# Lightning attention and an ELU mixture layer on one core: a third transpose buffer, a reordered block 11 and 12, a split last product, and output stores merged over two sequences

## The chip, the core and the metric

The kernel runs on one core of one Trainium2 chip. The metric is the device time of one execution in microseconds (us), lower is better. The kernel before takes 210.24 us, the median of three runs (209.36 to 210.96).

## What is computed

Attention with a decay per head, in blocks of 64 positions, and behind it a two-layer network with an ELU. The inputs are `q`, `k`, `v` of 4 sequences x 8 heads x 768 positions x 64, one decay `lam` per head, `w_in` of 512x2048 and `w_out` of 2048x512, all float32. Cut to what matters:

```
for b in range(nb):                       # nb = 12 blocks of 64 positions
    intra = (q_b @ k_b.T * Dmask) @ v_b   # Dmask: lam ** (i - j), lower half
    inter = (q_b * lam_pow) @ kv_state
    out_b = intra + inter
    kv_state = lam_block * kv_state + (k_b * rev_pow).T @ v_b
x = out.transpose(0, 2, 1, 3).reshape(4 * 768, 512)
h = x @ w_in
g = where(h > 0, h, exp(min(h, 0)) - 1)
return g @ w_out                          # 3072 x 512, float32
```

## The kernel before

**Blocks and groups.** The work is cut into 24 *blocks* `s` (0 to 23). Block `s` holds 64 positions of two neighbouring sequences, one on partitions 0 to 63, the other on 64 to 127: `where(s)` (L50) gives the first sequence, `2 * (s % 2)`, and the chunk of positions, `s // 2`. The state of block `s` is needed by block `s + 2`. Two blocks make one *group* of 256 rows; the two-layer network runs by groups.

**A block's attention.** `load` (L65) brings `k`, `q` and `v` from DRAM on POOL's queue, with a cast to fp16, in two DMAs each, one per sequence. Blocks 0 to 9 have `k` and `q` transposed on TensorE. From block 10 on `dma_T` (L234) does it with two DMA transposes on SP's queue, into a tile `TD` that has two buffers. `decay_q` (L205) scales the transposed `q` (tile `qs`), `decay_s` (L196) the state of the block two before (`sd`), `decay_v` (L187) the values (`vd`). `visit` (L278) issues the small matmuls of one block: state times `qs` (L304), scores of the *next* block from `TD` (L328), the state's update (L320), scores times values (L313). `att_P` (L214) masks the scores, `att_N` (L256) adds the update to `sd` and so makes the new state, `att_X` copies the block's output to `xt`, the input of the network.

**The network.** `mm1_h` (L377) computes one of eight units of a group's hidden layer: 8 matmuls of 128x256 into a PSUM bank `psH` (two buffers). `elu` (L420) makes `g` of it in one of two forms: for group 3 and units 0 to 4 of group 4, ACT reads the bank twice (L395, L397) and DVE combines two SBUF tiles (L402); for the rest ACT computes relu and exp (L429, L431) and DVE reads the bank itself (L432). Groups 0 to 2 have the second layer as plain products (`mm2`, L447), copied out by ACT in `mm2_o` (L457). Later groups use a form with seven half-size products (`part`, L516): each of 8 matmuls of 128x256 at L508, with sums of `g` (L490) and of the weights (L478) on DVE, and with `keep` (L535, ACT), `add` (L540, DVE) and `c2` (L544, DVE) to collect the output tile `o` (four buffers).

**Stores.** An output tile `o` of a block is 128 rows x 512 float32, 64 rows for each of two sequences, which lie 768 rows apart in DRAM. Each store is two DMAs of 64 rows (L461 in `mm2_o`, L527 in `store`), nearly all on SP's queue, in program order with the DMA transposes. Only at the end `c2` and the last `store` put one of their two halves on ACT's queue (L703, L706).

**What sets the order.** The order on each engine is written out by hand: a string of words for the first part (L565 to L579), and from L601 a loop over groups 3 to 11 and units `u` 0 to 7. A visit is made at `u` 1 and 5, so that group 4 has visits 10 and 11. Loads are issued at `u` 0 and 4, four blocks ahead. Block 11's decays are on DVE: `decay_s` at (4, 2), `decay_q` at (4, 3). From block 12 on both are on POOL, ahead of the visit before (L616, L617), behind all the loads that were issued until then. The last group's second layer stands by itself from L680 to L706.

Of the kernel before, what the change touches and what calls it, by code (L numbers as in the profile page):

```python
# [8 lines left out]
FP32 = mybir.dt.float32  # L9
# [7 lines left out]
def kernel(  # L17
# [35 lines left out]
    def half(x):  # L53
        return slice(64 * x, 64 * x + 64)
# [10 lines left out]
    def load(which, s):  # L65
        b, c = where(s)
        src, keep, tag = {"k": (k, kn, "kn"), "q": (q, qn, "qn"), "v": (v, vn, "vn")}[which]
        keep[s] = inp.tile([128, H, D], FP16, tag=tag, bufs=NB, name=f"{tag}{s}")
        for r in range(2):
            nc.gpsimd.dma_start(  # L70
                out=keep[s][half(r)],
                in_=src[b + r, :, c * L : (c + 1) * L, :].rearrange("h p d -> p h d"),
            )
# [122 lines left out]
    def decay_s(s, eng):  # L196
        if not NPR <= s < NS - NPR:
            return
        st[s]["sd"] = asb.tile([128, 2, NHP, D], FP32, tag="sd", bufs=3, name=f"sd{s}")
        eng.tensor_tensor(  # L200
            out=st[s]["sd"][:], in0=state[s - NPR][:],
            in1=lamL[:].unsqueeze(1).unsqueeze(3).broadcast_to([128, 2, NHP, D]), op=ALU.mult,
        )
# [18 lines left out]
    def att_C(s):  # L222
        if s >= NT:
            return
        T = asb.tile([128, 2, NHP, 2, L], FP16, tag="T", bufs=4, name=f"T{s}")
        to, psT = T[:].rearrange("p i j r t -> p r (i j) t"), st[s].pop("psT")
        if isinstance(psT, list):
            for r in range(2):
                nc.vector.tensor_copy(to[:, r], psT[r].rearrange("p (x t) -> p x t", t=L))
        else:  # L230
            nc.vector.tensor_copy(to, psT.rearrange("p r (x t) -> p r x t", t=L))
        st[s]["T"] = T

    def dma_T(s):  # L234
        if not NT <= s < NS:
            return
        T = asb.tile([128, 2, NHP, 2, L], FP16, tag="TD", bufs=2, name=f"TD{s}")
        for i, src in enumerate((kn, qn)):
            nc.sync.dma_start_transpose(
                out=T[:, i].rearrange("p j r t -> p j (r t)"),  # L240
                in_=src[s][:].rearrange("p h d -> p (h d)"),
            )
        st[s]["T"] = T
# [12 lines left out]
    def att_N(s):  # L256

        if s >= NS - NPR:
            return
        b, c = where(s)  # L260
        state[s] = asb.tile([128, 2, NHP, D], FP16, tag=f"st{b}", bufs=2, name=f"st{s}")
        to = state[s][:].rearrange("p y j d -> p y (j d)")
        if c:
            nc.vector.tensor_tensor(  # L264
                out=to, in0=psU, in1=st[s]["sd"][:].rearrange("p y j d -> p y (j d)"), op=ALU.add
            )
        else:
            nc.vector.tensor_copy(to, psU)
# [151 lines left out]
    def elu(grp, u):  # L420

        psH, nb, T, name = unit[grp, 0, 2, u]
        if grp == 3 or grp == 4 and u < 5:
            mm1_e(grp, 0, 2, u)
            mm1_g(grp, 0, 2, u, NF2)
            return

        r = msb.tile([128, nb, T], FP32, tag="r", bufs=4, name=f"r{name}")
        nc.scalar.activation(r[:], psH[:], AF.Relu, scale=-1.0)  # L429
        e = msb.tile([128, nb, T], FP32, tag="e", bufs=4, name=f"e{name}")  # L430
        nc.scalar.activation(e[:], r[:], AF.Exp, scale=-1.0)  # L431
        nc.vector.scalar_tensor_tensor(  # L432
            out=place(grp, 0, 2, u, 2, NF2), in0=e[:], scalar=-1.0, in1=psH[:],
            op0=ALU.add, op1=ALU.max,
        )
# [1 line left out]
    acc = {}  # L437
    nacc = [0]

    def rows(s, r):  # L440

        b, c = where(s)
        r0 = (b + r) * S + c * L
        return out[r0 : r0 + L, :]


    def mm2(s, n0):  # L447
        if n0 == 0:
# [8 lines left out]
    def mm2_o(s):  # L457
        o = msb.tile([128, DM], FP32, tag="o", bufs=4, name=f"o{s}")
        nc.scalar.copy(out=o[:], in_=acc.pop(s))
        for r in range(2):  # L460
            nc.sync.dma_start(out=rows(s, r), in_=o[half(r), :])  # L461

# [57 lines left out]
        }[i]  # L522
        product_of(grp, i, d[bank][:, cols], first, i in (4, 2, 3, 7))

    def store(s, o, cols, queues=(nc.sync, nc.sync)):
        for r in range(2):
            queues[r].dma_start(out=rows(s, r)[:, cols], in_=o[half(r), cols])  # L527

    def out_tile(grp, c):
        d = res[grp]  # L530
        if c not in d:
# [9 lines left out]
        o = out_tile(grp, c)[:, cols]  # L541
        nc.vector.tensor_tensor(out=o, in0=src, in1=res[grp][kept][:], op=ALU.add)

    def c2(grp, queues=(nc.sync, nc.sync)):  # L544
        d = res[grp]
        nc.vector.tensor_tensor(
            out=out_tile(grp, 1)[:].rearrange("p (i t) -> p i t", i=2),
            in0=d["A"][:, HD:].unsqueeze(1).broadcast_to([128, 2, HD]), in1=d["c45"][:].rearrange("p (i t) -> p i t", i=2), op=ALU.add,
        )
        store(2 * grp + 1, d[1], slice(0, DM), queues)  # L550

    def consts(i):
        if i == 0:
# [47 lines left out]
    for grp in range(3, NG):  # L601
        old, new = grp - 2, grp - 1
        for u in range(8):
            mm1_h(grp, 0, 2, u, NF2)
            s = 2 * grp + 2 + u // 4
            if s < NS and u % 4 == 0:

                if nload < NS:
                    load("k", nload)
                    load("q", nload)  # L610
                if nload <= NS:
                    load("v", nload - 1)
                    nload += 1
            if s < NS and u % 4 == 1:
                if s != 10:
                    decay_q(s + 1, nc.vector if s < 10 else nc.gpsimd)  # L616
                    decay_s(s + 1, nc.vector if s < 10 else nc.gpsimd)  # L617
                visit(
                    s, s if s < NS - NPR else None, s + 1 if s + 1 < NS else None,
                    s + 2 if s + 2 < NT else None,  # L620
                )
                dma_T(s + 3)

            if (grp, u) in five:
                mm2(5, 4 * five.index((grp, u)))
            end = grp == NG - 1
            if old >= 3 and u in (0, 2):
                part(old, {0: 3, 2: 7}[u])
            if new >= 3:
                at_u = {1: 2, 3: 4, 4: 1, 5: 5, 6: 6, 7: 3} if end else {3: 2, 4: 1, 5: 4, 6: 5, 7: 6}  # L630
                if u in at_u:
                    part(new, at_u[u])

            if old >= 3 and u == 1:
                add(old, 0, hi, res[old]["A"][:, hi], "p35")
                store(2 * old, res[old][0], slice(0, DM))
            if old >= 3 and u == 0:
                g_sum(old, 3)
            if new >= 3 and u in (4, 5, 6):
                g_sum(new, {4: 1, 5: 2, 6: 4}[u])  # L640
            if end and u == 3:
                g_sum(new, 3)
            if new >= 3 and u == 4:
                add(new, 0, lo, res[new]["A"][:, hi], "p2")
            if s + 1 < NS:
                if u % 4 == 1:
                    att_P(s + 1)
                if u % 4 == 2:
                    att_C(s + 2)
                    att_N(s)  # L650
                if u in (3, 7) and grp > 3:
                    decay_v(s + 1, nc.vector)
                if (grp, u) == (4, 2):
                    decay_s(s + 1, nc.vector)
                if (grp, u) == (4, 3):
                    decay_q(s + 1, nc.vector)
            if old >= 3 and u == 2:
                c2(old)
            if (grp, u) == (5, 0):
                w_sum(3, 1)  # L660
            elu(grp, u)
            if grp == 3 and u in (3, 6):
                decay_v(s + 1, nc.vector)
            if s < NS and u % 4 == 1:
                att_X(s, nc.scalar)
            if old >= 3 and u == 0:
                keep(old, "p35", res[old]["B"][:, hi])
            if new >= 3 and u == (1 if end else 3):
                keep(new, "p2", res[new]["B"][:, lo])
            if new >= 3 and u == (5 if end else 6):  # L670
                keep(new, "c45", res[new]["B"][:])
            if end and u == 6:
                keep(new, "u2", res[new]["A"][:, hi], 1)
            if end and u == 7:
                add(new, 0, hi, res[new]["B"][:, hi], "u2")
                store(2 * new, res[new][0], slice(0, DM))
            if (grp, u) == five[-1]:
                mm2_o(5)
# [20 lines left out]
    product_of(G, 2, M[1][:, lo], True, True)  # L699
    add(G, 0, lo, M[1][:, lo], "u1")  # L700
    store(2 * G, d[0], lo)
    part(G, 7)
    c2(G, (nc.sync, nc.scalar))  # L703
    part(G, 3)
    add(G, 0, hi, HB[:, hi], "u2")
    store(2 * G, d[0], hi, (nc.scalar, nc.sync))  # L706


# [28 lines left out]
```

## Time and profile before

| | |
|---|---|
| median of 3 runs | 210.24 us |
| the profiled execution's own time | 210.27 us |
| its span, from first to last instruction | 208.5 us |
| granted TensorE clock | 1.00 |
| TensorE (PE) busy | 91% of the span |
| VectorE (DVE) busy | 83% |
| ScalarE (ACT) busy | 68% |
| GpSimd (POOL) busy | 63% |
| last DVE instruction ends | 204.6 us into the span |

How to read the profile: times are us from the start of the span, those marked ns are nanoseconds. PE is the matmul array, PEld its weight load, SPq and ACTq are the instruction queues of SyncE and ScalarE where they issue DMAs. A group line names the line of the kernel, the engine, the operation, the tile written and the tiles read, the count behind an x, then busy time and mean ns of one, then the idle time in front and what ended it. A DMA's "us to landing" runs from its issue until its data is there. The share of a DMA queue is the time that its packets took, over the time of all 16 DMA engines; packets of one engine overlap, so that a share may be above 100%.

### The profile page before, as it was taken

The page shows a single profiled execution, that of the slowest core. Times are in us where ns is not written, and L with a number is a line of the kernel's source. Part 1 is how long each engine was busy: PE and PEld are TensorE (multiplying, and loading weights), DVE is VectorE, ACT ScalarE, POOL GpSimd, SP SyncE. Part 2 cuts the span into 40 slices and gives each one's busy share as a digit, 9 for nine tenths or more (in the row PEclk, how much of TensorE's full clock was granted, in tenths as well). Part 3 has the DMA queues.
Part 4 walks back from the last instruction along what each step waited for, and adds up shares of the span by engine and source line. Part 5 has one row for each costly group of instructions (what it writes and reads, how often), then busy time and mean ns, then how long its engine had stood idle before and what let it go on. Part 6 is the DMA issues. An engine that isn't in the chain of part 4 may idle for free.

```text
span 208.5 us, 7848 instructions
## 1 busy us (share of the span) xinstructions
PE 190.2 (91%) x3352; PEld 158.1 (76%) x3352; DVE 172.1 (83%) x281; ACT 140.7 (68%) x265; POOL 132.0 (63%) x180
## 2 busy tenths in 40 slices
PE   0448989999999999989999999999999999999991
PEld 0347977846776777868888888888888888888880
DVE  3677596798989898999989999999979956758672
ACT  5314686741784878767878778778788688877820
POOL 8978933899899879964999999999412200000000
PEclk9999999999999999999999999999999999999999
DMA  6999999999999999999999999999924404004043
GB/s 103 145 152 134 169 200 196 179 118 170 109 148 153 168 115 162 114 74 108 126 170 90 151 163 72 190 116 91 189 29 57 101 0 105 5 6 94 3 101 101
DMA packets 99731, 24.38 MB, mean 117 GB/s; under 512 B 92400, under 2 KB 96752, under 8 KB 99696
## 3 DMA queue, kind: packets, MB, share of 16 engines
q0 software_dynamic: 78208, 13.38, 96.0%
q1 hardware_dynamic: 20128, 10.03, 25.5%
q10 hardware_dynamic: 1360, 0.46, 1.2%
q8 instruction: 26, 0.43, 0.8%
q14 instruction: 9, 0.07, 0.1%
HBM read 27.27 MB, written 6.29 MB: 161 GB/s over the span
## 4 chain that ended last, share of the span: by engine, by line
PE 83%; DVE 6%; POOL 3%; DMA 3%; issue 2%; ACT 1%; DVEq 0%; POOLq 0%
PE psH L385 40%; PE psM L508 22%; PE psM L452 10%; DMA wi<-in_moe_w_in_dram 3%; PE psO_None L304 2%; PE psZ L328 2%; POOL vn L70 1%; DVE g L432 1%; PE psO_None L313 1%; PE psHA L508 1%; PE psHB L508 1%; PE psZ L320 1%; DVE s L490 1%; DVE vd L191 1%; DVE P L217 1%
## 5 line engine op out<-in xcount | busy, mean ns | idle before, releaser
L385 PE MATMUL psH<-xt,wi 128*128 128x256 f16 (+1 forms) x960 | 101.8, 257 | 2.6 <-DMA wi<-in_moe_w_in_dram 1.7
L385 PEld LDWEIGHTS <-wi 128*128 128x128 f16 x960 | 80.7, 101 | 13.7 <-issue 2.7
L432 DVE SCALAR_TENSOR_TENSOR g<-e,psH 128x512 f16<-128x512 f32 x59 | 40.2, 682 | 12.5 <-ACT e L431 12.1
L429 ACT ACTIVATE r<-psH 128x512 f32<-128x512 f32 x59 | 35.2, 597 | 21.5 <-PE psH L385 21.4
L431 ACT ACTIVATE e<-r 128x512 f32<-128x512 f32 x59 | 37.2, 630 | 1.9
L70 POOL DMA_DIRECT2D qn<-in_q_dram x46 | 32.4, 727 | 5.3 <-issue 2.7
L70 POOL DMA_DIRECT2D vn<-in_v_dram x48 | 34.0, 734 | 2.6 <-DMA qn<-in_q_dram 1.0
L395 ACT ACTIVATE e<-psH 128x512 f32<-128x512 f32 x37 | 22.2, 599 | 19.1 <-PE psH L385 18.8
L70 POOL DMA_DIRECT2D kn<-in_k_dram x46 | 32.5, 725 | 2.3 <-DMA wo<-in_moe_w_out_dram 2.3
L508 PEld LDWEIGHTS <-s 128*128 128x128 f16 x288 | 28.1, 98 | 3.4
L402 DVE SCALAR_TENSOR_TENSOR g<-e,r 128x512 f16<-128x512 f32 x37 | 26.1, 713 | 5.2 <-ACT r L397 5.2
L209 POOL TENSOR_TENSOR qs<-TD,powi 128x512 f16<-128x512 f16 x12 | 15.8, 1316 | 17.3 <-PE psO_None L304 12.4
L508 PE MATMUL psM<-wt,s 128*128 128x256 f16 x192 | 24.9, 273 | 0.0
L452 PE MATMUL psM<-wo,g 128*128 128x512 f16 x96 | 23.9, 380 | 0.0
L508 PEld LDWEIGHTS <-g 128*128 128x128 f16 x216 | 20.5, 98 | 2.6
L397 ACT ACTIVATE r<-psH 128x512 f16<-128x512 f32 x37 | 22.1, 598 | 0.0
L191 DVE TENSOR_TENSOR vd<-vn,rev 128x512 f16<-128x512 f16 x22 | 19.6, 891 | 0.0
L217 DVE TENSOR_TENSOR P<-psZ,mask 128x512 f16<-128x512 f32 x24 | 16.4, 684 | 2.6 <-PE psZ L328 2.0
L508 PE MATMUL psM<-wo,g 128*128 128x256 f16 x136 | 17.6, 273 | 0.0
L252 ACT CAST xt<-psO_None 128x512 f16<-128x512 f32 x20 | 11.5, 577 | 6.2 <-PE psO_None L313 6.2
L264 DVE TENSOR_TENSOR st<-psZ,sd 128x512 f16<-128x512 f32 x20 | 13.7, 683 | 0.9 <-PE psZ L320 0.9
L200 POOL TENSOR_TENSOR sd<-st,lamL 128x512 f32<-128x512 f16 x10 | 13.4, 1345 | 1.4 <-DVE st L264 1.4
(77 smaller groups left out, 207.0 us busy)
## 6 DMA issues: line engine op xcount, KB each, us to landing
out_dram<-o SPq DMA_DIRECT2D x45, 128.0 KB, 3.4
vn<-in_v_dram POOLq DMA_DIRECT2D x48, 64.0 KB, 4.6
kn<-in_k_dram POOLq DMA_DIRECT2D x46, 64.0 KB, 4.5
qn<-in_q_dram POOLq DMA_DIRECT2D x46, 64.0 KB, 4.9
wi<-in_moe_w_in_dram POOLq DMA_DIRECT2D x8, 256.0 KB, 5.8
wo<-in_moe_w_out_dram POOLq DMA_DIRECT2D x4, 512.0 KB, 7.7
kraw<-in_k_dram SPq DMA_DIRECT2D x2, 128.0 KB, 4.1
qraw<-in_q_dram ACTq DMA_DIRECT2D x2, 128.0 KB, 4.5
```

The costliest lines, as they stand in the source:

```text
L70: nc.gpsimd.dma_start(out=keep[s][half(r)], in_=src[b + r, :, c * L : (c + 1) * L, :].rearrange("h p d -> p h d"),)
L191: eng.tensor_tensor(out=st[s]["vd"][:], in0=vn[s][:], in1=rev[:].unsqueeze(2).broadcast_to([128, H, D]), op=ALU.mult,)
L217: nc.vector.tensor_tensor(out=d["P"][:].rearrange("p y j t -> p y (j t)"), in0=psS, in1=mask[:].rearrange("p y j t -> p y (j t)"), op=ALU. ...
L385: nc.tensor.matmul(psH[:, i, :], lhsT=wi[n // 4][:, kk, (n % 4) * 128 : (n % 4 + 1) * 128], rhs=xt[grp][:, kk, c0 * 128 : c0 * 128 + T], s ...
L395: nc.scalar.activation(e[:], psH[:], AF.Exp)
L397: nc.scalar.activation(r[:], psH[:], AF.Relu)
L402: nc.vector.scalar_tensor_tensor(out=place(grp, c0, nc_, n0, nb, step), in0=e[:], scalar=-1.0, in1=r[:], op0=ALU.add, op1=ALU.min,)
L429: nc.scalar.activation(r[:], psH[:], AF.Relu, scale=-1.0)
L431: nc.scalar.activation(e[:], r[:], AF.Exp, scale=-1.0)
L432: nc.vector.scalar_tensor_tensor(out=place(grp, 0, 2, u, 2, NF2), in0=e[:], scalar=-1.0, in1=psH[:], op0=ALU.add, op1=ALU.max,)
L452: nc.tensor.matmul(acc[s], lhsT=g_of(s, n), rhs=wo[n // 4][:, n % 4, :], start=(n == 0), stop=(n == NFT - 1),)
L508: nc.tensor.matmul(to, lhsT=lhsT, rhs=rhs, start=start and n == 0, stop=stop and n == NF2 - 1, skip_group_check=True,)
```

## The change

- `TD` gets three buffers.
- In group 4, `att_N(10)` stands at unit 1 in place of 2, and `decay_s(11)` behind `decay_q(11)` at unit 3 in place of 2. Unit 4 of group 4 takes the second form of the ELU.
- At (4, 4) POOL issues: load k of block 15, `decay_q(12)`, loads q 15, v 14 and k 16, `decay_s(12)`. Before it was k 15, q 15, v 14, `decay_q(12)`, `decay_s(12)`, and k 16 at (5, 0).
- Every store is one DMA: its source is 128 rows of a tile, its destination in DRAM 2 x 64 rows.
- The last product (part 3 of group 11) is made in two halves of 128 columns, the first into `HB`, the second into `M[1]` with a precomputed addend `w`; each has its own add. The last stores are one on ACT's queue (`c2`) and one on SP's.

```diff
-        T = asb.tile([128, 2, NHP, 2, L], FP16, tag="TD", bufs=2, name=f"TD{s}")
+        T = asb.tile([128, 2, NHP, 2, L], FP16, tag="TD", bufs=3, name=f"TD{s}")
...
-        if grp == 3 or grp == 4 and u < 5:
+        if grp == 3 or grp == 4 and u < 4:
...
-    def rows(s, r):
+    def store(s, o, cols, queue=nc.sync):
         b, c = where(s)
-        r0 = (b + r) * S + c * L
-        return out[r0 : r0 + L, :]
+        queue.dma_start(
+            out=out.rearrange("(b t) d -> b t d", b=B)[b : b + 2, c * L : (c + 1) * L, cols],
+            in_=o[:, cols],
+        )
...
-        for r in range(2):
-            nc.sync.dma_start(out=rows(s, r), in_=o[half(r), :])
+        store(s, o, slice(0, DM))
...
-    def store(s, o, cols, queues=(nc.sync, nc.sync)):
-        for r in range(2):
-            queues[r].dma_start(out=rows(s, r)[:, cols], in_=o[half(r), cols])
...
-                if nload < NS:
+                if (grp, u) == (4, 4):
                     load("k", nload)
+                    decay_q(s + 1, nc.gpsimd)
+                    load("q", nload)
+                    load("v", nload - 1)
+                    load("k", nload + 1)
+                    decay_s(s + 1, nc.gpsimd)
+                elif nload < NS:
+                    if grp != 5 or u:
+                        load("k", nload)
                     load("q", nload)
                 if nload <= NS:
-                    load("v", nload - 1)
+                    if (grp, u) != (4, 4):
+                        load("v", nload - 1)
                     nload += 1
             if s < NS and u % 4 == 1:
-                if s != 10:
+                if s not in (10, 11):
                     decay_q(s + 1, nc.vector if s < 10 else nc.gpsimd)
                     decay_s(s + 1, nc.vector if s < 10 else nc.gpsimd)
...
                 if u % 4 == 2:
                     att_C(s + 2)
+                if (grp, u) == (4, 1) or u % 4 == 2 and s != 10:
                     att_N(s)
...
-                if (grp, u) == (4, 2):
-                    decay_s(s + 1, nc.vector)
                 if (grp, u) == (4, 3):
                     decay_q(s + 1, nc.vector)
+                    decay_s(s + 1, nc.vector)
...
     store(2 * G, d[0], lo)
+    w = msb.tile([128, HD // 2], FP32, name="w")
+    nc.vector.tensor_tensor(
+        out=w[:], in0=d["u2"][:, HD // 2 :], in1=d["c45"][:, HD + HD // 2 :], op=ALU.add
+    )
     part(G, 7)
-    c2(G, (nc.sync, nc.scalar))
-    part(G, 3)
-    add(G, 0, hi, HB[:, hi], "u2")
-    store(2 * G, d[0], hi, (nc.scalar, nc.sync))
+    c2(G, nc.scalar)
+    for i, (bank, more) in enumerate(((HB, d["u2"][:, 0 : HD // 2]), (M[1], w[:]))):
+        c = slice(HD + i * HD // 2, HD + (i + 1) * HD // 2)
+        for n in range(NF2):
+            nc.tensor.matmul(
+                bank[:, c], lhsT=gs[G, 4][:, n, :], rhs=wo[2 + n // 4][:, n % 4, c],
+                start=i == 1 and n == 0, stop=n == NF2 - 1, skip_group_check=True,
+            )
+        nc.vector.tensor_tensor(out=out_tile(G, 0)[:, c], in0=bank[:, c], in1=more, op=ALU.add)
+    store(2 * G, d[0], hi)
```

More of the change, by code (lines that the diff above doesn't have):

```diff
@@ L542, in add, with c2 @@
         nc.vector.tensor_tensor(out=o, in0=src, in1=res[grp][kept][:], op=ALU.add)
-    def c2(grp, queues=(nc.sync, nc.sync)):
+    def c2(grp, queue=nc.sync):
         d = res[grp]
@@ L549, in c2 @@
         )
-        store(2 * grp + 1, d[1], slice(0, DM), queues)
+        store(2 * grp + 1, d[1], slice(0, DM), queue)
     def consts(i):
```

## The prediction

> **What bounds the kernel now.** I read the chain of waits first, then the waits around blocks 10 to 12, which the change reorders, then the DMA view by stretches, because every store changes its form, and last the chain at the end. The page and its chain:
>
> ```profile
> span 208.5 us, 7848 instructions
> ...
> PE 190.2 (91%) x3352; PEld 158.1 (76%) x3352; DVE 172.1 (83%) x281; ACT 140.7 (68%) x265; POOL 132.0 (63%) x180
> ...
> PE 83%; DVE 6%; POOL 3%; DMA 3%; issue 2%; ACT 1%; DVEq 0%; POOLq 0%
> ```
>
> TensorE bounds it: 83% of the chain, and the steady groups repeat every 14.7 us without a gap. The chain of the stretch 80 to 96 us leaves PE for DVE once, at visit 11 (PE would go on at 88.4) and the unit after it:
>
> ```profile
> 87.60 0.85 DVE vd L191
> 88.45 0.60 DVE qs L209
> ...
> 92.32 0.68 DVE g L432
> 93.00 0.05 issue
> 93.05 1.05 PE psH L385 x8
> ```
>
> The waits from 74 to 95 us say what PE loses there:
>
> ```profile
> PE psO_None L304 <- DVE qs L209: 0.7, 1, 0.7
> ...
> PE psH L385 <- DVE g L432: 0.5, 1, 0.5
> ```
>
> So the middle holds 1.2 us to be won. Now the DMA view. From 41 to 47 us only POOL's loads run:
>
> ```profile
> q0 software_dynamic: 5686, 0.71, 187.5%
> ```
>
> 5,686 packets in 6.0 us on 16 engines are 16.9 ns each; the share of 187.5% shows that packets overlap two deep, so shares are not occupancy. Then 45 to 85 us, and 85 to 152 us, where the loads end:
>
> ```profile
> q0 software_dynamic: 27814, 3.46, 159.4%
> q1 hardware_dynamic: 4144, 2.23, 29.9%
> ...
> out_dram<-o SPq DMA_DIRECT2D x12, 128.0 KB, 4.4
> ```
> ```profile
> q0 software_dynamic: 27939, 3.47, 109.2%
> q1 hardware_dynamic: 11679, 4.72, 39.2%
> ...
> out_dram<-o SPq DMA_DIRECT2D x16, 128.0 KB, 3.7
> ```
>
> Loads alone are 27,814 / 16 x 16.9 ns = 29.4 us of each engine in the first 40 us, and 29.5 us in the next 67. From 160 us on there are almost only stores:
>
> ```profile
> q1 hardware_dynamic: 2144, 2.56, 23.6%
> ...
> out_dram<-o SPq DMA_DIRECT2D x17, 128.0 KB, 2.4
> ```
>
> The chain's last pieces; the last add ends at 204.6, and 3.9 us of stores follow:
>
> ```profile
> 202.34 0.87 PE psHA L508 x8
> 203.21 0.89 PE psHB L508 x8
> ...
> 204.19 0.42 DVE o L542
> ```
>
> **The change, part by part.** The sum is made against the profiled execution's 210.27 us (208.5 of span, 1.8 around it), 0.03 above the median of 210.24.
>
> *Third buffer.* SP's queue waits 8.9 us for two `qs` reads on DVE: 3.5 before the transposes of block 12 (from 73.9 to 77.5) and 5.4 before block 13's (83.7 to 89.1). Both go. `TD` 12 can land near 81, 13 near 91 in place of 96.6. POOL's idle 4.7 us at 92 to 96.7 goes, but nothing on the chain waits for POOL there (that `qs` ends at 98.3, its visit is at 104.5): worth nothing by itself.
>
> *Block 11 on DVE.* Before `qs` 11 stood: masked scores, g, state, sd, g, vd. Now: masked scores, state, g, g, vd. One `sd` (0.60 apart in the timeline) goes behind it, so visit 11 starts up to 0.60 earlier; `sd` 11 is needed only at 93.5. The state 10 comes one g earlier, that g 0.6 later; it ends before 85, and g is read two groups of products later, so this costs nothing. Unit 4 in the other ELU form has DVE instead of ACT free the bank: 0 to 0.5 (the row above for unit 5); I take 0, DVE being ahead by the 0.6.
>
> *Block 12 on POOL.* `qs` 12 moves ahead of loads q 15, v 14 (2.7 us of issue) and of k 16 (1.4, from behind `sd` 12). At 82.0 it would wait if `TD` 12 is late; with the third buffer it lands at about 81, so nothing; without cover it costs what holds four to six loads, up to the 2.9 us by which it lands later today (84.9), hidden by the loads' lead below. `sd` 12 (1.5) comes after k 16, near 88, still 9 us before its update. DVE instructions beside today's 84.9 to 87.9 pair of POOL took 1.65 and 1.52 in place of 0.68; such lengthening moves, it doesn't go. I take the two waits, 0.6 + 0.5 = 1.1, as gained; bounds 0 and 1.8.
>
> *Last product.* 16 matmuls of 128 columns for 8 of 256: the 128-column row runs 16 in 0.89 us, beside 0.87, so 0. The first add runs beside the second half; the last add is 128 columns, about 0.3 for 0.42; `w` (0.3) lies under the product before. One issue of 0.55 goes from each queue. Together 0.3 gained; bounds 0 and 0.9.
>
> *Merged stores.* 24 tiles, 128 rows per DMA instead of 64. No row shows this form: every transfer of the trace has an outermost count of 64 or 128 on both sides, and each 64-row store leaves 64 packets of 2,048 bytes and 16 closing ones of 4 bytes in the trace's DMA records. The new destination's outermost loop counts 2, with a jump of 768 rows. Lower bound: spread over 16 engines as now, one issue of about 0.59 us less per tile on SP, which is idle: 0. Upper bound: one engine per sequence, two in all. Then a tile is 64 rows on each. In the trace's DMA records such rows follow 80 ns apart on an engine with nothing else to do: 5.1 us. The last stretch's share gives the other end: 23.6% of 16 x 48.5 us for 2.56 MB is 18.7 us of engine time per 0.262 MB, 9.4 on each of two, but with overlap counted twice. I take two engines and 5.1. The reason is a judgement on form: to stay on 16, the transfer would have to be cut inside a loop whose outer step jumps, and a cut along the outermost loop accounts for all that the rows show.
>
> On two engines this has two prices. *Loads:* both engines must carry 29.4 + 6 tiles x 5.1 + 6 transposes x 0.5 (32 packets of some 16 ns) = 63 us in the first 40, and 29.5 + 8 x 5.1 + 22 x 0.5 = 81 in the next 67: 37 too much. Loads have a lead of 8 us (block 12: issued at 67.2, its scores at 89.1, less 1.4 + 4.7 + 2.5 + 4.9 for issue and landing of load and transpose) to 13 (block 14, likewise); I take 11. Transposes stand behind the stores on SP's queue, so the rest shows as `visit` waiting for `TD`: +27. *The end:* from 200.6 (the store issued at 198.6, 2 us to its data) come three full tiles and two half-row ones: 3 x 5.1 + 2 x 64 x 46 ns = 21.3 us, ending at 222.6 with its completion: +14.
>
> The sum: 210.3 + 27 + 14 - 1.1 - 0.3 = 249.9, so 250 us. With 9.4 per tile the same steps give 327, too far up for rows that overlap; with 6.7 (105 ns, the spacing beside other traffic) 279.
>
> The Trainium skill, "DMA: Bandwidth & Descriptors", section "Why a DMA increments its semaphore by 16 and not by 1", says that a transfer uses the largest number of engines up to 16 that divides both sides' outermost counts, which here is 2. By it the sum stays 250; by the row of 64-row stores alone it would be 209. The same page's "Rules for kernel authors" advises one 128-partition transfer instead of two on disjoint halves, which by itself speaks for the merge; no run shown here tells the two apart.
>
> **Rivals.**
>
> *Only the end is hurt* (25%). Two engines, but loads keep going ahead of stores and transposes ahead of need. For it: output tiles have four buffers, so stores may lag two groups; a steady group has 14.7 us for 10.2 of stores. Against: the first stretch is over by 23 us, and transposes queue behind stores. 210.3 + 14 - 1.4 = 223.
>
> *Sixteen engines, the other side* (25%). The store is spread as now; then only the waits and the last product count: 210.3 - 1.4 = 208.9, not slower. It decides from eight engines on: 16 rows each, 1.3 us a tile, 14 x 0.6 more on each engine, which both stretches can hold (29 of 40 us used). For it: nothing in the trace runs on fewer engines. Against: nothing in it has an outermost count of 2.
>
> *POOL is held up* (within the last): `TD` 12 is late, POOL stands at `qs` 12 with q 15, v 14 and k 16 behind it, whose transposes wait. Up to 2.9, less the 8 of lead: 0, and visible only as POOL idle. No chance of its own.
>
> **How the numbers follow.** The forecast (two engines, loads delayed) has 50%, its own range 237 to 279 (from a lead of 13 with two stores in arrears, 37 - 13 - 10 = 14 in place of 27, to rows 105 ns apart). About 1%, 2.1 us, is what a measurement of this kernel can tell from no change. Sixteen engines: 208.9 is 0.7% below, so of its 25% I give 15 to within 1%, 9 to faster (a gain of over 2.1 needs the upper bounds 1.8 and 0.9), 1 to slower. Slower: 50 + 25 + 1 = 76%. The range must reach to sixteen engines to leave no more than 2 in 10 out: 208 to 270 holds some 42 + 25 + 20.
>
> **What would show it.** Right: the stores' time to landing 8 us or more where it is 3.4 now, loads and transposes above 6; PE waiting for `TD` from visit 9 on; the last add near 236 and 15 to 18 us from it to the end. The middle: PE's waits for `qs` 11 and g gone, SP's wait for `qs` gone. Wrong: stores landing in 3 us. If they land late but TensorE's steady group stays 14.7, it is 223.

## The result

The changed kernel takes 272.98 us, the median of 4 runs, beside 210.03 for the kernel before. The ratio is 1.281, with a 95% interval of 1.268 to 1.295: 59 us slower. Single executions of a kernel can come out a few per cent longer than the others: ratios leave those out, while medians, spreads and some traces include them (the trace below is one of 278.31 us, where the ratio rests on 267.88 and 270.50). So prices are taken from ratios, and the trace is read for places and shares.

### The profile page after: what moved, and what is told of

It reads as the page before. It is cut to its first block, busy times and chain, and to the rows that moved or that the text cites. A ratio compares the mean times of both kernels' runs of the same rounds, so it can differ in the third digit from the quotient of the medians.

```text
span 276.5 us, 7824 instructions
## 1 busy us (share of the span) xinstructions
PE 205.2 (74%) x3360; PEld 166.0 (60%) x3360; DVE 172.9 (63%) x283; ACT 141.9 (51%) x265; POOL 131.3 (47%) x180
## 4 chain that ended last, share of the span: by engine, by line
PE 43%; DMA 26%; POOL 10%; issue 9%; DVE 3%; ACT 1%; SPq 0%; POOLq 0%
PE psH L385 20%; PE psM L508 18%; DMA wo<-in_moe_w_out_dram 7%; DMA vn<-in_v_dram 7%; DMA TD<-qn 4%; DMA kn<-in_k_dram 3%; POOL qn L70 3%; POOL kn L70 3%; POOL vn L70 3%; DMA wi<-in_moe_w_in_dram 2%; DMA qn<-in_q_dram 2%; DVE s L490 1%; POOL wi L88 1%; PE psO_None L304 1%; PE psHA L508 1%
## 5 line engine op out<-in xcount | busy, mean ns | idle before, releaser
L385 PE MATMUL psH<-xt,wi 128*128 128x256 f16 (+1 forms) x960 | 109.0, 268 | 4.1 <-DMA wi<-in_moe_w_in_dram 2.2
L385 PEld LDWEIGHTS <-wi 128*128 128x128 f16 x960 | 84.6, 105 | 18.9 <-issue 5.4
L432 DVE SCALAR_TENSOR_TENSOR g<-e,psH 128x512 f16<-128x512 f32 x60 | 40.9, 682 | 17.0 <-ACT e L431 16.4
L70 POOL DMA_DIRECT2D qn<-in_q_dram x46 | 32.0, 711 | 24.5 <-DMA kn<-in_k_dram 20.3
L508 PEld LDWEIGHTS <-s 128*128 128x128 f16 x280 | 28.9, 104 | 4.8
L402 DVE SCALAR_TENSOR_TENSOR g<-e,r 128x512 f16<-128x512 f32 x36 | 24.4, 686 | 8.9 <-ACT r L397 8.9
L508 PE MATMUL psM<-wt,s 128*128 128x256 f16 x192 | 27.8, 293 | 0.0
L191 DVE TENSOR_TENSOR vd<-vn,rev 128x512 f16<-128x512 f16 x22 | 16.9, 770 | 13.9 <-DMA vn<-in_v_dram 13.9
L453 PE MATMUL psM<-wo,g 128*128 128x512 f16 x96 | 25.6, 400 | 0.0
L335 PEld LDWEIGHTS <-qn 64*64 64x64 f16 x160 | 3.2, 125 | 24.0 <-DMA qn<-in_q_dram 11.0
L320 PE MATMUL psZ<-vd,kn 64*64 64x64 f16 x352 | 7.6, 201 | 11.1 <-issue 10.9
```

The lines of the kernel that those rows point to most:

```text
L70: nc.gpsimd.dma_start(out=keep[s][half(r)], in_=src[b + r, :, c * L : (c + 1) * L, :].rearrange("h p d -> p h d"),)
L191: eng.tensor_tensor(out=st[s]["vd"][:], in0=vn[s][:], in1=rev[:].unsqueeze(2).broadcast_to([128, H, D]), op=ALU.mult,)
L385: nc.tensor.matmul(psH[:, i, :], lhsT=wi[n // 4][:, kk, (n % 4) * 128 : (n % 4 + 1) * 128], rhs=xt[grp][:, kk, c0 * 128 : c0 * 128 + T], s ...
L402: nc.vector.scalar_tensor_tensor(out=place(grp, c0, nc_, n0, nb, step), in0=e[:], scalar=-1.0, in1=r[:], op0=ALU.add, op1=ALU.min,)
L432: nc.vector.scalar_tensor_tensor(out=place(grp, 0, 2, u, 2, NF2), in0=e[:], scalar=-1.0, in1=psH[:], op0=ALU.add, op1=ALU.max,)
L453: nc.tensor.matmul(acc[s], lhsT=g_of(s, n), rhs=wo[n // 4][:, n % 4, :], start=(n == 0), stop=(n == NFT - 1),)
```

## The profile after

The page: TensorE's share of the span falls from 91% to 74%, and of the chain from 83% to 43%. In its place stand DMA, POOL and "issue", which is time in front of an instruction for which the profile shows no releaser.

```profile
span 276.5 us, 7824 instructions
...
PE 205.2 (74%) x3360; PEld 166.0 (60%) x3360; DVE 172.9 (63%) x283; ACT 141.9 (51%) x265; POOL 131.3 (47%) x180
...
PE 43%; DMA 26%; POOL 10%; issue 9%; DVE 3%; ACT 1%; SPq 0%; POOLq 0%
```

The chain from 20 to 104 us says which transfers are late. A load of `v` takes 19.4 us where the median was 4.6, and the second transpose of block 11 (`TD<-qn`) 12.1:

```profile
49.15 19.43 DMA vn<-in_v_dram
...
75.57 9.23 DMA kn<-in_k_dram
84.81 0.03 issue
84.83 0.02 POOLq L70
84.85 0.49 issue
85.34 5.07 DMA qn<-in_q_dram
90.41 0.35 SPq L239
90.76 0.04 issue
90.80 0.03 SPq L239
90.83 0.03 issue
90.86 12.09 DMA TD<-qn
```

TensorE's first new wait is for `q` of block 7, which it transposes at L335 and whose loads were issued at 47.8 and 48.5 us. Later in the trace it stands in the middle of visits for something that the profile doesn't name (from the waits of the whole run; L320 is the state's update):

```profile
PE psO L335 <- DMA qn<-in_q_dram: 10.8, 2, 7.6
...
PE psZ L320 <- issue: 10.9, 2, 5.5
```

The DMA view of 45 to 85 us: 15,067 packets of loads in place of 27,814 in the same 40 us, and loads that need twice their time. The merged stores have no time to landing in this view, so they are followed by their packets below.

```profile
q0 software_dynamic: 15067, 1.87, 121.0%
q1 hardware_dynamic: 1034, 1.17, 14.3%
...
kn<-in_k_dram POOLq DMA_DIRECT2D x12, 64.0 KB, 10.3
qn<-in_q_dram POOLq DMA_DIRECT2D x11, 64.0 KB, 10.2
```

The end: the last add stops at 257.5, and 19.0 us of stores follow in place of 3.9. From 258 us on, the DMA view has a flat rate of about 50 GB/s, which is what two engines give with a row of 2,048 bytes each 80 ns (51 GB/s); the fullest slices of the kernel before, with the same tiles, have some 200 GB/s.

```profile
257.18 0.29 DVE o L723
```
```profile
GB/s 53 53 53 44 53 53 53 44 53 53 53 53 44 53 53 53 49 49 53 53 53 47 53 49 46 51 47 49 49 49 49 49 49 49 46 49 20 0 0 0
```

Visits by the start of their last matmuls (L313), us, from the traces; the last five rows belong to the experiments below:

| kernel | visit 5 | 6 | 9 | 11 | 12 | 22 | 23 | last add ends | span |
|---|---|---|---|---|---|---|---|---|---|
| before | 55.7 | 62.1 | 76.7 | 89.5 | 98.0 | 171.8 | 178.3 | 204.6 | 208.5 |
| changed | 55.7 | 76.0 | 96.9 | 113.9 | 123.3 | 224.8 | 231.4 | 257.5 | 276.5 |
| e3, merged at the end only | 55.5 | 61.9 | 76.4 | 88.5 | 98.6 | 172.1 | 178.6 | 204.8 | 223.6 |
| e7, all stores on ACT's queue | 55.9 | 85.4 | 105.8 | 118.1 | 128.4 | 218.3 | 227.2 | 255.8 | 274.6 |
| e9, merged for blocks 0 to 5 | 55.9 | 74.4 | 93.9 | 107.4 | 119.9 | 195.0 | 201.6 | 227.7 | 231.7 |
| e10, merged for blocks 6 to 19 | 55.0 | 61.3 | 76.2 | 88.2 | 99.5 | 201.4 | 207.9 | 234.0 | 238.0 |
| e11, split and first ELU form | 57.4 | 63.8 | 78.6 | 90.7 | 102.7 | 176.2 | 182.7 | 208.8 | 212.9 |

Three places: 14 us at once between visits 5 and 6 and 11 more up to visit 12, then groups of 20.3 us on average ((224.8 - 123.3) / 5) where they were 14.8, and the end.

## The experiments

Theory: a merged store runs on two DMA engines, which delays loads and transposes in the middle and the closing stores at the end. Rivals: the reordering of blocks 11 and 12 is to blame; only the end is hurt; it is not the count but the jump in the destination, or the number of DMAs, that makes stores slow.

**Which part of the change it is: e1 and e2.** e1 is the changed kernel with each store as two DMAs again:

```diff
-        queue.dma_start(
-            out=out.rearrange("(b t) d -> b t d", b=B)[b : b + 2, c * L : (c + 1) * L, cols],
-            in_=o[:, cols],
-        )
+        for r in range(2):
+            r0 = (b + r) * S + c * L
+            queue.dma_start(out=out[r0 : r0 + L, cols], in_=o[half(r), cols])
```

> The changed kernel with one thing undone: each store is again two DMAs of 64 rows. Theory (a merged store runs on two DMA engines): all of the loss goes, 208 to 210 us, stores land in about 3 us and leave 16 closing packets each. Rival (the reordering of blocks 11 and 12 or the third buffer makes POOL and the loads late): it stays above 250 us.

Measured: 211.05, ratio 0.998 (0.993 to 1.002), so all of the loss goes; it is a little above the 208 to 210 expected, because the small gains of the change aren't there either. e2 is the kernel before with the opposite edit, the merged store and nothing else but the queues of the last two stores.

> The kernel before with the merged store alone; c2's last store on ACT's queue, the last one on SP's. Theory: about the changed kernel's time, 262 to 278 us, TensorE waiting for k, q and TD from about 50 us on. Rival (the reordering): 209 to 212 us.

Measured: 273.58, ratio 1.278 (1.265 to 1.291). The merged store is the whole loss, within the intervals, and the rest of the change is worth nothing that can be measured.

**Middle and end: e3 and e4.** Both are the changed kernel; `store` merges only under a condition, and else issues the two DMAs of e1:

```diff
+        if s >= 20:        # e3; e4: s < 20
             queue.dma_start(
                 out=out.rearrange("(b t) d -> b t d", b=B)[b : b + 2, c * L : (c + 1) * L, cols],
                 in_=o[:, cols],
             )
+            return
```

> The changed kernel, stores merged for blocks 20 to 23 alone. Theory: the loads' price goes and the end's stays, the last add at 203 to 205 us and 15 to 19 us behind it, 221 to 226 us in all. Rival (the end is hidden, all the loss is in the middle): 208 to 211 us.

Measured: 225.40, ratio 1.067 (1.060 to 1.074), so 14.2 us (12.6 to 15.7) for the end. The chain stops as early as in the kernel before, and two engines work on alone: in the DMA view from 205 us on the rate is again flat.

```profile
204.46 0.29 DVE o L728
```
```profile
GB/s 53 48 48 53 53 53 44 53 53 53 53 53 44 53 53 53 53 44 53 53 53 53 44 51 53 48 48 48 48 48 48 46 48 48 48 48 46 2 0 0
```

> The changed kernel, stores merged for blocks 0 to 19 alone. Theory: the end's 14 to 16 us go, the loads' price stays: 250 to 260 us, with 4 to 6 us behind the last add. Rival (only the end is hurt): 208 to 211 us.

Measured: 252.59, ratio 1.191 (1.180 to 1.203), so 40 us (38 to 43) for the middle. Together 54 of the 59, equal within the intervals. The rival that only the end is hurt falls.

**Count or jump: e5 and e6.** The kernel before, each 64-row store cut into two row ranges, so that there is no jump in any destination: 62 and 2 rows in e5, 32 and 32 in e6 (the stores in `mm2_o` likewise).

```diff
         for r in range(2):
-            queues[r].dma_start(out=rows(s, r)[:, cols], in_=o[half(r), cols])
+            for i, e in ((0, 62), (62, 64)):    # e6: 32, e8: 49
+                queues[r].dma_start(out=rows(s, r)[i:e, cols], in_=o[64 * r + i : 64 * r + e, cols])
```

> The kernel before, each 64-row store cut into 62 and 2 rows: four DMAs per tile, none of them with a jump in its destination. Theory A (the count of the outermost loop sets the engines: 62 = 2 x 31, so two): 64 rows per tile on each of two engines as in the changed kernel, 255 to 285 us, two closing packets per DMA. Theory B (the two-level destination with its jump is what makes a store slow): 209 to 214 us.

Measured: 273.84, the median of three runs (269.34 to 277.15), which is the changed kernel's time, without its store and without its reordering.

> The control of the run above: each 64-row store cut into 32 and 32 rows, so as many DMAs, but 32 = 16 x 2. Both theories: 209 to 213 us, 16 closing packets per DMA. If it is slow as well, it is the number of DMAs on SP's queue that costs.

Measured: 211.88, ratio 1.004 (1.001 to 1.008). Twice the DMAs cost 0.9 us; cutting the same rows as 62 and 2, counts whose largest divisor up to 16 is 2, costs 58 to 66. It is the count. The DMA views of e5 and e6 show the same stores, the first ones without a time to landing, the second ones landing in 2.8 us:

```profile
out_dram<-o SPq DMA_DIRECT2D x45, 124.0 KB
```
```profile
out_dram<-o SPq DMA_DIRECT2D x90, 64.0 KB, 2.8
```

The packets of four bytes, which close a DMA, count the engines. On SP's queue the 28 transposes (32 each) and the two first loads (16 each) make 928 in every kernel, and e7 below, which has no store on this queue, has just these 928. The rest belongs to the stores:

| kernel | four-byte packets on SP's queue | stores there | closing packets of one |
|---|---|---|---|
| before | 1,696 | 48 | 16 |
| changed | 976 | 24 | 2 |
| e5 | 1,120 | 48 of 62 rows, 48 of 2 | 2 and 2 |
| e6 | 2,464 | 96 of 32 rows | 16 |
| e8 | 1,984 | 48 of 49 rows, 48 of 15 | 7 and 15 |

**How many engines are enough: e8.**

> The kernel before, each 64-row store cut into 49 and 15 rows. By the count rule 7 and 15 engines, so 7 engines carry 16 rows per tile, 1.3 us, where 4 rows per engine are usual per 64-row store. Theory A: 209 to 214 us, since both stretches can hold 0.6 us more per tile. Rival (any uneven spread delays the loads): above 216 us.

Measured: 211.92, ratio 1.006 (1.001 to 1.010), no worse than e6 with as many DMAs. The table fits 7 and 15 engines: 48 x (7 + 15) + 928 = 1,984. So a tile of 16 rows on each of seven engines is free here, and 64 rows on each of two are not.

**Queue or engines: e7.** The changed kernel with all merged stores on ACT's queue:

```diff
-    def store(s, o, cols, queue=nc.sync):
+    def store(s, o, cols, queue=nc.scalar):
...
-    def c2(grp, queue=nc.sync):
+    def c2(grp, queue=nc.scalar):
```

> The changed kernel with all merged stores on ACT's queue, so that no transpose stands behind a store on SP's queue. If the loads' price comes from loads that share two engines with the stores: 255 to 280 us as before, k, q and v landing late. If it comes from transposes behind stores in one queue: 225 to 240 us, the end's 15 us left.

Measured: 276.34, ratio 1.311 (1.300 to 1.323). By its total the first theory would hold, but the trace has other waits than the changed kernel's:

```profile
ACT xt L252 <- DMA TD<-kn: 20.7, 1, 20.7
...
PE psH L385 <- DVE g L432: 18.2, 15, 1.9
```

A store now stands in front of ACT's own work: between 56.3 and 77.0 us ACT does nothing but issue one (at 76.5), and visit 6 comes 29.5 us after visit 5, where it was 20.3. From visit 12 to 22, on the other hand, a group takes 18.0 us and not 20.3, and TensorE's waits in the middle of visits shrink from 17.4 us to 2.3; what it waits for there is `g`, which comes late from ACT. So with no transpose behind a store the groups do get faster, by 2.3 us each, and what is left of their loss has a new cause in it. The total agrees with the first theory by coincidence: the run doesn't separate the sharing of the two engines from the order in one queue.

**Where the middle's 40 us arise: e9 and e10.** As e3, with the conditions `s < 6` and `6 <= s < 20`.

> The changed kernel, stores merged for blocks 0 to 5 alone (the first stretch). By the prediction's sum (23 us too much, less the lead): 217 to 225 us. If loads give way to stores on the two engines row for row, six tiles of 6.7 us hold them nearly as long: 228 to 245 us.

> The changed kernel, stores merged for blocks 6 to 19 alone. By the prediction's sum (14.5 us too much, less 11 of lead): 210 to 216 us. If loads give way row for row: 222 to 240 us. With the run before, the two prices should add up to the 42 us of the run without the end.

Measured: 233.49 for e9 (three runs, 228.13 to 234.93), 17 us by the lowest and up to 24; 239.81 for e10, ratio 1.138 (1.129 to 1.147), 29 us (27 to 31). e9 is beyond the first theory's 225 at its lowest, e10 far beyond its 216; both lie in the range of "row for row", e9 near its lower end and e10 at its upper. The sum, 46 or more, is above e4's 40, so the two overlap in part.

**What the rest of the change does: e11 and e12.** e1 with the ELU condition back at `u < 5`; e12 has also the halves of the last two stores on both queues.

> The changed kernel with two DMAs per store and unit 4 of group 4 in the first ELU form again. If that form took back what the new order of block 11 gave: TensorE's wait for g near 92 us shrinks from 1.6 to under 0.6, and it takes 207.5 to 209.5 us, a ratio of 0.985 to 0.995. If not: 0.995 to 1.003.

> As the run before, and the last two stores have a half each on SP's and on ACT's queue again, as in the kernel before. One issue of 0.55 us less in a row at the end: 0 to 0.6 us faster than the run before.

Measured: e11 211.92, ratio 1.003 (1.000 to 1.007); e12 212.11, ratio 1.000 (0.996 to 1.005). Neither beats the kernel before, the two can't be told apart, and the wait near 92 us did not shrink. It is 0.46 us before. In e3, which up to the end has e1's form, TensorE stands 1.56 us for the `g` of unit 4, whose bank DVE frees now in place of ACT; in e12, with unit 4 in the first form again, it stands 1.84 us for the `g` of unit 5, as before (from the timelines of e3 and of e12):

```profile
91.40 1.05 PE L385 MATMUL psH<-xt,wi 128*128 128x256 f16 x8 [1.56 <-DVE g L432]
```
```profile
94.45 1.05 PE L385 MATMUL psH<-xt,wi 128*128 128x256 f16 x8 [1.84 <-DVE g L432]
```

The reason is in DVE's list of work up to that `g`. First the kernel before, then e12:

```profile
85.35 1.65 DVE L402 SCALAR_TENSOR_TENSOR g<-e,r 128x512 f16<-128x512 f32 x1
86.93 1.52 DVE L191 TENSOR_TENSOR vd<-vn,rev 128x512 f16<-128x512 f16 x1
88.38 0.68 DVE L209 TENSOR_TENSOR qs<-TD,powi 128x512 f16<-128x512 f16 x1
...
92.32 0.67 DVE L432 SCALAR_TENSOR_TENSOR g<-e,psH 128x512 f16<-128x512 f32 x1
```
```profile
87.80 0.68 DVE L209 TENSOR_TENSOR qs<-TD,powi 128x512 f16<-128x512 f16 x1
88.40 1.55 DVE L200 TENSOR_TENSOR sd<-st,lamL 128x512 f32<-128x512 f16 x1
...
91.41 1.19 DVE L402 SCALAR_TENSOR_TENSOR g<-e,r 128x512 f16<-128x512 f32 x1
...
93.72 0.67 DVE L432 SCALAR_TENSOR_TENSOR g<-e,psH 128x512 f16<-128x512 f32 x1
```

From the start of `qs` 11 to the start of that `g` DVE needs 5.9 us in e12 and 3.9 before. `sd` 11, which was moved behind `qs` 11, is 0.6 of the difference; the rest is that `sd` and a `g` take 1.55 and 1.19 us in place of 0.68. Before, two instructions were long as well (1.65 and 1.52), but ahead of `qs` 11. POOL works beside the long ones in both kernels:

```profile
88.06 1.39 POOL L70 DMA_DIRECT2D vn<-in_v_dram  x2
...
90.75 1.29 POOL L200 TENSOR_TENSOR sd<-st,lamL 128x512 f32<-128x512 f16 x1
```

That POOL's work lengthens DVE's is only read from times side by side. Not every instruction beside POOL is long: in the kernel before none of DVE's is from 88.4 to 92 us, while POOL issues loads. No run took the third buffer or the order of POOL's work away by itself, so their parts aren't shown.

## Why the prediction was right, and which terms were not

**The total.** The forecast was 250 us. By the ratio the changed kernel takes 269 (1.281 x 210.24), at the very top of the stated 208 to 270, and the median of its four runs, 272.98, lies above. The range was drawn so as to reach down to the rival at 209; that its upper end just holds the result is luck. Of a loss of 59 us it had 41 in its terms. The direction and the mechanism were right, and the size of the largest term was not.

**The merged store on two engines: right.** Closing packets, the flat 50 GB/s, and e5 without any jump show it. The reason given, a cut along the outermost loop, was a judgement, at even chances; the experiments bear it out. The Trainium skill, "DMA: Bandwidth & Descriptors", section "Why a DMA increments its semaphore by 16 and not by 1", has the largest count up to 16 that divides both outermost counts; the runs agree for 2, 7, 15 and 16 engines, and it also says that each engine used posts one closing increment, which is what the table counts. The advice of the same page to use one 128-partition transfer for two disjoint halves does not hold here: the merge by itself costs 28% (e2).

**The end, 14 us: right.** e3 has 14.2. Rows of 2,048 bytes alone on an engine start 80 ns apart (from every second row of the last stretch, median), as taken.

**The loads, 27 us: the mis-sized term.** Measured: 40 (e4). (From its own figures, 37 too much less a lead of 11, it would be 26.) The step that failed is the lead, which was to hide 11 us. It was read from blocks 12 and 14, but the first stretch's stores meet the loads of blocks 6 to 9. In the kernel before, the second `q` load of these blocks is issued 5.9, 8.2, 9.4 and 10.0 us before TensorE transposes it, and a `q` load takes 5.4 us to land there, so their lead is 0.5 to 4.6 us. e9's 17 to 24 us fit the over-demand of 23 with no more than such a lead taken off.

For the second stretch the sum had 14 us too much, over a fixed 67 us with 8 tiles, and the lead was to cover most of it. e10 has 29: five groups of 20.4 us, 5.6 more than before, and nothing of that is hidden. An estimate of what each of the two engines carries in one group is 2 tiles x 64 rows x 80 ns + 12 loads x 32 x 16.9 ns + 4 transposes x 0.5 = 10.2 + 6.5 + 2.0 = 18.7 us, 3.9 of these 5.6. It is no exact bound, since e7 moves the same rows in groups of 18.0.

The path that the prediction named, visits that wait for `TD`, is there: in e5 it is the longest of TensorE's waits. The loss begins earlier, though, with the 10.8 us for `q` of block 7, which no `TD` holds.

```profile
PE psZ L328 <- DMA TD<-qn: 20.7, 5, 7.0
```

**Gains, 1.1 and 0.3 us: not there.** With the store undone, the rest is worth nothing that can be measured (e1). The step "the two waits, 0.6 + 0.5 = 1.1, as gained" failed. The first wait is gone, and visit 11 comes 1.0 earlier (e3: 88.5 for 89.5), but the second grew from 0.5 to 1.6 in e3 and 1.8 in e12, and visit 12 comes 0.6 later (e3: 98.6 for 98.0). `sd` 11 was taken away from in front of `qs` 11 and put in front of the `g` that TensorE waits for next. The prediction had noted that DVE's lengthening moves and doesn't go, and that unit 4's other form can cost up to 0.5; it took nothing for either. That the small gains don't show in the total is measured; that DVE's list is the reason is read from the traces. The last product gained 0.2 of its 0.3 (from visit 23 to the last add's end 26.3 before, 26.1 in e3).

**The rivals.** Sixteen engines: falls; with split stores (e1) it would indeed have been 210 to 211. Only the end: falls by e4. POOL held up at `qs` 12 by a late `TD`: not seen; in e1 and e3 POOL waits 1.0 and 0.7 us there, and the profile puts it down to ACT.

Of the signs, the last add "near 236" doesn't follow from the prediction's own sum, which puts it at 230 (204.6 + 27 - 1.4); in the trace it is 257.5, and 19.0 us of stores follow for the 15 to 18 forecast.

Open: how the loss of the groups divides into shared engines, transposes behind stores in one queue, and TensorE's clock. For the clock there is an estimate: from visit 12 to 22 TensorE's matmuls take 81.8 us in e10 at a granted clock of 0.90, and 75.5 in e7 at 1.00, so it is directly some 6 of e10's 29 us.

## What to carry to other kernels

Before two DMAs are merged into one, look at the outermost count on both sides: 128 rows against 2 x 64 use two engines, and the transfer is as slow as its share on one of them. A store that nothing waits for can still hold up the kernel, because loads and transposes beside it and behind it land late (loads here 8 to 11 us in place of 4.5 to 4.9); count the rows per engine of all queues together against the period of the loop. A lead hides such a delay only for the loads that have it: read it at each stretch. And work that is moved out of the way of one wait stands in front of the next one: follow the engine's list up to that one before you call a wait gained.

## What the runs showed of the hardware that was not expected

**Stores and loads alternate.** In the changed kernel's first burst, three tiles, 192 rows on each of two engines, take 20.3 us: 105.8 ns per row, where they start 80 ns apart (median) in the last groups, when the loads are over. That leaves some 25 ns a row for load packets, which alone take 16.9 ns each. In the same time the 16 engines carry 5,826 load packets, 364 each on average, so at most about two go with a row, where an engine without stores carries six in that time. One to two per row is an estimate, as the records don't name the engine. It fits the Trainium skill, "DMA: Bandwidth & Descriptors", section "Queues, rings and completion order", by which an engine takes its queues in turn, packet by packet.

**TensorE's clock.** In the changed kernel TensorE waits for 5.5 us from 157.5, and the next matmuls run at half speed (the timeline, then its windows with PE's and the others' busy times, granted clock, DMA share and GB/s):

```profile
163.63 1.89 PE L385 MATMUL psH<-xt,wi 128*128 128x256 f16 x8
165.31 1.91 PE L508 MATMUL psM<-wt,s 128*128 128x256 f16 x8
167.02 1.81 PE L385 MATMUL psH<-xt,wi 128*128 128x256 f16 x8
168.66 1.04 PE L508 MATMUL psM<-wo,g 128*128 128x256 f16 x8
```
```profile
163.40:168.80 5.40, 5.40 (x49) 3.90 (x41) 3.42 (x6) 1.81 (x3) 4.13 (x6) 0.52 2.64 128
168.80:175.00 6.20, 6.20 (x116) 5.41 (x114) 5.20 (x9) 4.52 (x9) 6.20 (x8) 1.00 5.03 116
```

Three sets of eight matmuls start 1.7 us apart in place of 0.87, so a wait of 5.5 us costs some 8. In the traces' clock records each stretch at half speed, up to the last matmuls, is a whole number of steps of 3.41 us: here two, from 161.8 to 168.6. In e11 a wait of 2.56 us was followed by one such step:

```profile
96.32 1.89 PE L385 MATMUL psH<-xt,wi 128*128 128x256 f16 x8 [2.56 <-DVE g L432]
98.00 1.73 PE L507 MATMUL psM<-wt,s 128*128 128x256 f16 x8
99.56 1.04 PE L385 MATMUL psH<-xt,wi 128*128 128x256 f16 x8
```

The waits of 1.56 us in e3 and 1.84 in e12 were followed by none. The Trainium skill, "TensorE: Matmul & The Clock Gate", section "Part 1: The HAM clock gate (the "warmup" mystery)", has half rate after an idle window of about 3.4 us and about as long to come back, with windows that run freely. The steps of 3.41 us agree; e11's wait is shorter than a window, and TensorE was busy for 1.16 of the 3.4 us ahead of its slow step.
